# Softplus of the first feed-forward: the logarithm tile in two PSUM banks, in turn, in place of SBUF

## The chip, the cores and the metric

One core of one Trainium2 chip runs the whole program. The metric is the time of one execution on the device in microseconds (us); the median of three runs counts.

## The reference, cut to what matters

```python
x = attention(q, k, v, s)                                  # 2304 tokens x 512
h = x @ w_in                                               # 512 -> 2048
g = np.maximum(h, 0.0) + np.log1p(np.exp(-np.abs(h)))      # softplus
x = g @ w_out                                              # 2048 -> 512
xn = x / sqrt(mean(x * x) + 1e-06) * rms_g
out = (silu(xn @ w_gate) * (xn @ w_val)) @ w_out2          # 512 -> 1536 -> 512
```

Matrices reach TensorE as pairs of a rounded high part and a remainder, and every product is three matmuls: high by high, low by high, high by low.

## The kernel before

The program has three stages: attention (to about 315 us), the first feed-forward (to about 794 us) and the second one (to the end). All instructions are recorded in an order that the kernel sets itself: each kind of work has an offset (the tables `OFF`, `OFF1`, `OFF2`), work item number n stands at n plus its offset, and one sort gives the order of every engine's queue. An engine takes its queue strictly in that order.

The first feed-forward works in 96 steps i. A step is one tile of 384 tokens and one block of 128 hidden columns. The first 36 steps do six blocks for each of the six tiles; the other 60 do the ten remaining blocks of each tile. Each step is a chain over three engines, and the letters are used below:

- **h** (PE, `m1_h`, L642 to L644): 12 matmuls of 384 columns into one PSUM bank. The bank comes from the pair `p`, and in every third step from the bank `x1`, so three banks take turns.
- **A, X, U, LN** (ACT, L661, L665, L673, L669): absolute value of h, exp(-|h|), 1+e rounded, and ln(1+e) into the tile `l`, which lies in SBUF and has two buffers.
- **D** (DVE, L677): e becomes (u-1)-e, the rounding error of U, from two SBUF tiles.
- **G** (DVE, L681): e becomes max(h,0)-e, from PSUM and SBUF. It is the last reader of h and frees its bank.
- **AD** (DVE, L685): l becomes l+e, both in SBUF.
- **GH** (ACT, L689) and **GL** (DVE, L694): the high half of l, and the remainder l-gh. In the first six steps GL runs on POOL.
- **Y** (PE, `m1_y`): 12 matmuls with gh and gl, adding into four PSUM banks that a tile keeps over its blocks.

By the offsets the queues read as follows. PE: h(i), Y(i-3), h(i+1), Y(i-2), ... ACT: A(i), X(i), U(i), LN(i), GH(i-1), A(i+1), ... DVE: D(i), GL(i-1), G(i), AD(i), D(i+1), ... Between these stand the conversions of the weights of both feed-forwards from float64, one chunk in about 1.5 steps: ACT L232 and L234, DVE L241 (some chunks), L242, L244 and L246, POOL L252, then for the chunks kept on chip a split (ACT L278, POOL or DVE L284). POOL also splits the inputs (L639) and does the squares and scaling of the norm (L739 to L773).

After the last block of a tile its norm is made: `m1_ssum` (PE, L753 and L754, two matmuls into the bank `o0`), then `m1_inv` (DVE L762 reads `o0`; ACT L763 and L764 take logarithm and exponential; POOL L765 to L768). Five of the six norms fall into the first feed-forward. Before the change nothing else uses `o0` in this stage.

Of the kernel before, what the change touches and what calls it, by code (L numbers as in the profile page):

```python
# [15 lines left out]
ALU = mybir.AluOpType  # L16
# [98 lines left out]
    "ss": 0.96675,  # L115
    "sr": 0.57611,
    "sh": 4.36453,
    "sm": 6.76979,
    "iv": 7.36353,
    "xn": 8.20666,  # L120
    "xr": 0.64747,
    "sh5": 4.81356,
# [18 lines left out]
def attention_moe_kernel(ctx, tc, q, k, v, s, w_in, w_out, w_gate, w_val, w_out2, rms_g, out):  # L141
    nc = tc.nc
# [9 lines left out]
    T = 384  # L152
# [7 lines left out]
    FA = 6  # L160
# [16 lines left out]
    def ps_p(name):  # L177
        return ps.tile([P, 512], F32, tag="p", name=name, bufs=2)

    def ps_1(tag, w=512):  # L180
        return ps.tile([P, w], F32, tag=tag, name=tag, bufs=1)

    def f32(ap):
        return ap.bitcast(F32)
# [11 lines left out]
    ypd = [dram.tile([DM, T], F32, tag=f"yp{t}", name=f"yp{t}") for t in range(NTILE)]  # L196
    xnT = [dram.tile([DM, T], F32, tag=f"xn{t}", name=f"xn{t}") for t in range(NTILE)]

# [1 line left out]
    slots = {}  # L200
    wfd = [dram.tile([2 * F1, P, 512], F32, tag="wf1", name="wf1"),
           dram.tile([3 * F2, P, 512], F32, tag="wf2", name="wf2")]
# [80 lines left out]
        eng = nc.vector if ph == 1 and c >= NA and c % 4 == 3 else nc.gpsimd  # L283
        eng.tensor_tensor(out=w[1], in0=raws.pop((ph, c)), in1=f32(w[0]), op=ALU.subtract)  # L284

# [1 line left out]
    st = {}  # L287

    def setup():
# [189 lines left out]
    def a_n4(p):  # L479
        scale_rows(st["e4", p], st["r4", p])  # L480

    # groups of transposed blocks: (key block, query blocks); the first two feed float32 products
    GRP = [
        [(0, [0, 1, 2])],
        [(1, [1, 2]), (2, [2])],
# [85 lines left out]
    def on_pair(fn, hd):  # L571
# [25 lines left out]
        "XL": lambda: x_load0(),  # L597
        **{f"X{a}": (lambda a=a: x_split(0, a, nc.vector)) for a in range(KD)},
        "H0": lambda: m1_h(0), "H1": lambda: m1_h(1),
    }  # L600

# [1 line left out]
    def x_tile():  # L603
        return pools["m1"].tile([P, T], F32, tag="xr", name="xr", bufs=2)

# [35 lines left out]
    def mm3(o, wh, wl, xh, xl, start, stop):  # L641
        nc.tensor.matmul(o, wh, xh, start=start, stop=False)  # L642
        nc.tensor.matmul(o, wh, xl, start=False, stop=False)  # L643
        nc.tensor.matmul(o, wl, xh, start=False, stop=stop)  # L644

    def m1_h(i):
        v, _, f = STEPS[i]
        w = slots[1, 2 * f]
        xh, xl = [st["xh", v, a] for a in range(KD)], [st["xl", v, a] for a in range(KD)]
        h = ps_1("x1") if i % 3 == 2 else ps_p("h")  # L650
        for a in range(KD):
            c = slice(a * P, (a + 1) * P)
            mm3(h[:, 0:T], w[0][:, c], w[1][:, c], xh[a], xl[a], a == 0, a == KD - 1)
        st["h", i] = h[:, 0:T]

    def m1_tile(tag, bufs, dt=F32):
        return pools["m1"].tile([P, T], dt, tag=tag, name=tag, bufs=bufs)
# [7 lines left out]
        nc.scalar.activation(out=e, in_=e, func=AF.Exp, scale=-1.0)  # L665

    def m1_ln(i):
        l = st["l", i] = m1_tile("l", 2)
        nc.scalar.activation(out=l, in_=st["e", i], func=AF.Ln, bias=1.0)  # L669

    def m1_u(i):
# [18 lines left out]

    def m1_gl(i):
        gl = st["gl", i] = m1_tile("gl", 3, F32R)
        eng = nc.gpsimd if i < FA else nc.vector
        eng.tensor_tensor(out=gl, in0=st.pop(("l", i)), in1=f32(st["gh", i]), op=ALU.subtract)  # L694

    def m1_y(i):
        v, _, f = STEPS[i]
# [75 lines left out]
        nc.gpsimd.tensor_tensor(out=y, in0=y, in1=st["inv", t], op=ALU.mult)  # L773
        nc.sync.dma_start(out=xnT[t][a * P:(a + 1) * P], in_=y)

# [1 line left out]
    def n_load(t, a):  # L777
        xr = st["xr", t, a] = x_tile()
        nc.sync.dma_start(out=xr, in_=xnT[t][a * P:(a + 1) * P])
# [51 lines left out]
                    nc.vector.tensor_copy(out=ob, in_=o[m][:, c])  # L831
                nc.sync.dma_start(out=out[r:r + P, c], in_=ob)

# [1 line left out]
    with tc.manual_schedule():  # L835
        nc.scalar.preload_act_table_set("natural_log_exp_and_others")
        with ExitStack() as es:
# [21 lines left out]
        with ExitStack() as es0:  # L859
# [8 lines left out]
            for i in NS:  # L868
                for nm, fn in (("h", m1_h), ("A", m1_abs), ("X", m1_exp), ("LN", m1_ln), ("U", m1_u), ("D", m1_d),
                               ("G", m1_g), ("AD", m1_add), ("GH", m1_gh), ("GL", m1_gl), ("Y", m1_y)):  # L870
                    if nm != "h" or i > 1:
                        at(i + OFF1[nm], fn, i)
# [8 lines left out]
            for v in sorted({STEPS[i][0] for i in NS}):  # L881
                i = min(i for i in NS if STEPS[i][0] == v)
# [74 lines left out]
```

## Time and profile before

| | |
|---|---|
| median of 3 runs | 1239.92 us (1238.71 to 1243.12) |
| span of the profiled execution | 1242.4 us |
| PE busy over the span | 1176.2 us (95%) |
| DVE busy | 771.7 us (62%) |
| ACT busy | 617.7 us (50%) |
| POOL busy | 471.5 us (38%) |

The profiled execution lies 2.5 us above the median. Busy shares are means over three stages with different limits, so a change inside the first feed-forward is read from that stage alone. In the 40 slices of the page DVE reads 9 tenths or more from slice 12 to slice 24 (about 370 to 780 us), and in the second feed-forward 3 or 4.

### The profile page before, as it was taken

What the parts mean: (1) busy time and instruction counts of PE and PEld (TensorE: products, weight loads), DVE (VectorE), ACT (ScalarE), POOL (GpSimd) and SP (SyncE); (2) the same over time, 40 slices, a digit from 0 to 9 for tenths busy, and PEclk for the clock granted to TensorE, in tenths of its full rate; (3) what the DMA queues carried; (4) which work ended last, traced back from release to release, by engine and by line L of the source; (5) the groups of instructions that cost most, each with busy time, mean ns of one, the idle gap of its engine ahead of it and who ended that gap; (6) DMA issues with size and microseconds to landing.
All of it is one profiled execution on the core that took longest, in us unless ns stands there. A gap on an engine that the chain in (4) does not pass through costs nothing.

```text
span 1242.4 us, 18308 instructions
## 1 busy us (share of the span) xinstructions
PE 1176.2 (95%) x6404; PEld 1042.1 (84%) x6404; DVE 771.7 (62%) x1396; ACT 617.7 (50%) x1467; POOL 471.5 (38%) x487
## 2 busy tenths in 40 slices
PE   4999999999999998999989879999999999999998
PEld 3677777776988888999888768899999999999997
DVE  4666676654699999998999999533333332333322
ACT  2667666665677777866666666442121121212111
POOL 4455655543354544346576776762000000000000
PEclk9999999999899998999999999999999999999999
DMA  9998888753333343544452332331101010010000
GB/s 181 198 192 178 200 193 186 167 131 100 99 129 119 122 139 123 162 140 134 159 165 91 120 101 85 117 97 58 39 14 39 14 39 1 14 39 13 26 1 26
DMA packets 139037, 128.96 MB, mean 104 GB/s; under 512 B 66656, under 2 KB 116352, under 8 KB 138912
## 3 DMA queue, kind: packets, MB, share of 16 engines
q1 hardware_dynamic: 138848, 127.74, 38.6%
q8 instruction: 51, 0.84, 0.3%
q14 instruction: 42, 0.34, 0.1%
q0 software_dynamic: 96, 0.04, 0.0%
HBM read 76.46 MB, written 26.12 MB: 83 GB/s over the span
## 4 chain that ended last, share of the span: by engine, by line
PE 67%; DVE 22%; ACT 4%; issue 3%; DMA 2%; SPq 2%; POOL 1%; DVEq 0%; POOLq 0%; ACTq 0%
DVE gl L694 5%; PE x L539 4%; PE pt L504 4%; PE g L644 4%; PE g L643 4%; PE v L644 4%; PE v L643 4%; PE v L642 4%; PE g L642 4%; PE o L530 4%; DVE l L685 4%; DVE e L677 3%; PE o L818 3%; PE o L819 3%; PE o L817 3%
## 5 line engine op out<-in xcount | busy, mean ns | idle before, releaser
L643 PE MATMUL y<-gl,w 128*128 128x384 f32 x384 | 134.5, 350 | 25.4 <-DVE gl L694 24.1
L252 POOL TENSOR_TENSOR wf<-ur 128x512 int32<-128x512 int32 x68 | 94.3, 1386 | 123.7 <-DVE ur L246 34.1
L802 DVE TENSOR_TENSOR u<-g,u 128x384 f32<-128x384 f32 x71 | 39.5, 556 | 158.9 <-ACT u L801 158.9
L642 PE MATMUL y<-gh,w 128*128 128x384 f32 x384 | 130.8, 341 | 3.1 <-ACT l L669 1.4
L644 PE MATMUL y<-gh,w 128*128 128x384 f32 x384 | 130.6, 340 | 0.0
L472 POOL TENSOR_SCALAR e<-e,r 128x256 f32<-128x256 f32 (+2 forms) x144 | 78.3, 560 | 127.9 <-ACT hl L368 103.1
L804 ACT ACTIVATE gh<-l 128x384 fp32r<-128x384 f32 x72 | 37.8, 524 | 156.0 <-DVE l L803 156.0
L801 ACT ACTIVATE u<-g 128x384 f32<-128x384 f32 x71 | 34.8, 490 | 151.9 <-PE g L644 151.8
L643 PEld LDWEIGHTS y<-gl,w 128*128 128x128 f32 x384 | 73.3, 191 | 36.7 <-DVE gl L694 35.1
L643 PE MATMUL g<-xl,w 128*128 128x384 f32 x284 | 95.6, 336 | 1.8 <-DVE xl L636 1.8
L689 ACT ACTIVATE gh<-l 128x384 fp32r<-128x384 f32 x96 | 49.9, 520 | 93.7 <-DVE l L685 93.5
L642 PE MATMUL g<-xh,w 128*128 128x384 f32 x284 | 95.8, 337 | 0.7 <-ACT xh L635 0.7
L694 DVE TENSOR_TENSOR gl<-l,gh 128x384 fp32r<-128x384 f32 x90 | 93.1, 1035 | 4.5 <-ACT gh L689 0.7
L644 PE MATMUL g<-xh,w 128*128 128x384 f32 x284 | 95.9, 338 | 0.0
L642 PE MATMUL h<-xh,w 128*128 128x384 f32 x256 | 89.2, 348 | 6.8 <-DVE e L681 6.6
L642 PE MATMUL v<-xh,w 128*128 128x384 f32 x284 | 94.9, 334 | 0.0
L644 PE MATMUL v<-xh,w 128*128 128x384 f32 x284 | 94.9, 334 | 0.0
L643 PE MATMUL v<-xl,w 128*128 128x384 f32 x284 | 94.9, 334 | 0.0
L643 PE MATMUL h<-xl,w 128*128 128x384 f32 x256 | 88.4, 345 | 3.5 <-POOL xl L639 3.3
L644 PE MATMUL h<-xh,w 128*128 128x384 f32 x256 | 87.4, 341 | 0.0
L685 DVE TENSOR_TENSOR l<-l,e 128x384 f32<-128x384 f32 x96 | 84.0, 875 | 3.7
L677 DVE SCALAR_TENSOR_TENSOR e<-u,e 128x384 f32<-128x384 f32 x96 | 73.9, 770 | 17.1 <-ACT l L669 17.1
(191 smaller groups left out, 3281.7 us busy)
## 6 DMA issues: line engine op xcount, KB each, us to landing
sk<-hl SPq DMA_DIRECT2D x96, 256.0 KB
raw<-in_moe_w_out_dram SPq DMA_DIRECT2D x28, 512.0 KB
raw<-in_moe_w_in_dram SPq DMA_DIRECT2D x16, 512.0 KB
raw<-in_moe_w_gate_dram SPq DMA_DIRECT2D x12, 512.0 KB
raw<-in_moe_w_val_dram SPq DMA_DIRECT2D x12, 512.0 KB
wf<-wf SPq DMA_DIRECT2D x24, 256.0 KB
wl<-wf SPq DMA_DIRECT2D x24, 256.0 KB
xr<-x SPq DMA_DIRECT2D x28, 192.0 KB
```

The costliest lines, as they stand in the source:

```text
L252: nc.gpsimd.tensor_tensor(out=w.bitcast(I32), in0=u, in1=r3, op=ALU.add)
L472: nc.gpsimd.tensor_scalar(out=e, in0=e, scalar1=r, scalar2=1.0, op0=ALU.mult, op1=ALU.mult)
L504: nc.tensor.transpose(t[:, o:o + P], e[:, EO[ib] + j0:EO[ib] + j0 + P], ident)
L530: nc.tensor.matmul(o[:, IS - w:IS], vn[:, jb, hd, :], x[:, c:c + w], start=(jb == 0), stop=(jb == 2))
L539: nc.tensor.matmul(t[:, 192 - w:192], vs[r, jb, 2 * hd:2 * hd + 2, :].rearrange("p a d -> p (a d)"), x[r, c:c + w], start=(i == 0 and jb = ...
L642: nc.tensor.matmul(o, wh, xh, start=start, stop=False)
L643: nc.tensor.matmul(o, wh, xl, start=False, stop=False)
L644: nc.tensor.matmul(o, wl, xh, start=False, stop=stop)
L677: nc.vector.scalar_tensor_tensor(out=e, in0=st.pop(("u", i)), scalar=-1.0, in1=e, op0=ALU.add, op1=ALU.subtract)
L685: nc.vector.tensor_tensor(out=l, in0=l, in1=st.pop(("e", i)), op=ALU.add)
L689: nc.scalar.activation(out=gh, in_=st["l", i], func=AF.Copy)
L694: eng.tensor_tensor(out=gl, in0=st.pop(("l", i)), in1=f32(st["gh", i]), op=ALU.subtract)
```

## The change

The tile `l` no longer lies in SBUF. LN writes it into a PSUM bank, `o0` in even steps and `x1` in odd ones; AD adds in place there; GH and GL read it there. Since POOL has no way to that memory in this kernel, GL is on DVE in all 96 steps. With `x1` taken, h has the two banks of `p` alone. The sum for the norm still uses `o0`, now between the logarithms of two even steps, and two offsets put the sum and the reading of it earlier (`sm`, `iv`).

```diff
-    "sm": 6.76979,
-    "iv": 7.36353,
+    "sm": 6.05,
+    "iv": 6.75,
...
-        h = ps_1("x1") if i % 3 == 2 else ps_p("h")
+        h = ps_p("h")
...
     def m1_ln(i):
-        l = st["l", i] = m1_tile("l", 2)
+        l = st["l", i] = ps_1(("o0", "x1")[i % 2])[:, 0:T]
...
         gl = st["gl", i] = m1_tile("gl", 3, F32R)
-        eng = nc.gpsimd if i < FA else nc.vector
-        eng.tensor_tensor(out=gl, in0=st.pop(("l", i)), in1=f32(st["gh", i]), op=ALU.subtract)
+        nc.vector.tensor_tensor(out=gl, in0=st.pop(("l", i)), in1=f32(st["gh", i]), op=ALU.subtract)
```

One line falls away, so L694 (GL) is L693 after the change and L762 (reading the sum) is L761.

On DVE the first steps of the stage read before, where GL is on POOL:

```order
L677 SCALAR_TENSOR_TENSOR e<-u,e 128x384
L681 SCALAR_TENSOR_TENSOR e<-h,e 128x384
L685 TENSOR_TENSOR l<-l,e 128x384
L677 SCALAR_TENSOR_TENSOR e<-u,e 128x384
L681 SCALAR_TENSOR_TENSOR e<-h,e 128x384
```

On DVE the same place after the change (names that begin with `o_` and `x_` are tiles in the banks `o0` and `x1`):

```order
L685 TENSOR_TENSOR o_4219<-o_4219,e 128x384
L677 SCALAR_TENSOR_TENSOR e<-u,e 128x384
L693 TENSOR_TENSOR gl<-o_4219,gh 128x384
L681 SCALAR_TENSOR_TENSOR e<-h,e 128x384
L685 TENSOR_TENSOR x_4247<-x_4247,e 128x384
```

One instruction a step is added to DVE's queue here, between D of a step and its G; from the seventh step on it stood there already.

On DVE around the first norm, before (`sq` is written from the sum, `ur` is a weight in conversion):

```order
L681 SCALAR_TENSOR_TENSOR e<-x_6889,e 128x384
L685 TENSOR_TENSOR l<-l,e 128x384
L242 TENSOR_SCALAR ur<-ur 128x512
L244 TENSOR_SCALAR ur<-ur 128x512
L246 SCALAR_TENSOR_TENSOR ur<-raw,ur 128x512
L677 SCALAR_TENSOR_TENSOR e<-u,e 128x384
L694 TENSOR_TENSOR gl<-l,gh 128x384
L762 TENSOR_SCALAR sq<-o_6984 128x384
L681 SCALAR_TENSOR_TENSOR e<-h,e 128x384
```

On DVE around the first norm, after the change:

```order
L685 TENSOR_TENSOR x_6954<-x_6954,e 128x384
L761 TENSOR_SCALAR sq<-o_6975 128x384
L242 TENSOR_SCALAR ur<-ur 128x512
L244 TENSOR_SCALAR ur<-ur 128x512
L246 SCALAR_TENSOR_TENSOR ur<-raw,ur 128x512
L677 SCALAR_TENSOR_TENSOR e<-u,e 128x384
L693 TENSOR_TENSOR gl<-x_6954,gh 128x384
L681 SCALAR_TENSOR_TENSOR e<-h,e 128x384
L685 TENSOR_TENSOR o_7019<-o_7019,e 128x384
```

The reading of the sum stands ahead of a conversion, of D and of GL, where it stood behind them. On ACT the two instructions that follow it (L763 and L764 before) move up by one step with it and stand again between A and X. On PE the two matmuls of the sum stand between the same neighbours as before, behind a Y and ahead of an h, at every norm.

## Rows read from the trace of the kernel before

**Rows 1.** Busy time by stretch; columns: us, then busy us (instructions) per engine.
```profile
core 0: us, PE busy (x) PEld busy (x) DVE busy (x) ACT busy (x) POOL busy (x), PEclk, DMA share, GB/s
336.50:475.50 139.00, 125.23 (x674) 117.35 (x673) 132.09 (x193) 101.05 (x215) 72.06 (x54) 0.98 0.38 124
475.50:534.90 59.40, 59.40 (x337) 59.40 (x337) 54.99 (x85) 47.35 (x99) 21.74 (x17) 0.98 0.50 161
534.90:767.30 232.40, 205.43 (x1114) 194.92 (x1114) 217.73 (x294) 152.09 (x316) 151.00 (x126) 0.99 0.38 121
767.30:794.30 27.00, 24.43 (x137) 23.39 (x136) 20.31 (x28) 16.91 (x34) 19.23 (x16) 1.00 0.45 138
```

**Rows 2.** Timeline of PE, one h and the Y behind it: start us, us, what.
```profile
501.63 0.33 PE L642 MATMUL h<-xh,w 128*128 128x384 f32 x1
...
503.71 0.33 PE L642 MATMUL y<-gh,w 128*128 128x384 f32 x1
```

**Rows 3.** Waits from 320 to 780 us: us in total, times, longest us.
```profile
PEld y L643 <- DVE gl L694: 35.1, 35, 3.7
...
PEld h L642 <- DVE e L681: 9.5, 9, 1.9
...
ACT acc L763 <- DVE sq L762: 6.7, 5, 2.0
```

**Rows 4.** Single lines: count, then ns minimum/median/maximum of one.
```profile
L694 DVE TENSOR_TENSOR gl<-l,gh x90: 545/852/1656, 349.5 to 785.4; 128x384 fp32r<-128x384 f32 x90
...
L685 DVE TENSOR_TENSOR l<-l,e x96: 557/796/1431, 322.6 to 783.7; 128x384 f32<-128x384 f32 x96
...
L677 DVE SCALAR_TENSOR_TENSOR e<-u,e x96: 544/552/1648, 321.4 to 780.1; 128x384 f32<-128x384 f32 x96
...
L681 DVE SCALAR_TENSOR_TENSOR e<-h,e x64: 541/546/560, 322.0 to 777.5; 128x384 f32<-128x384 f32 x64
...
L661 ACT ACTIVATE e<-h x64: 466/472/499, 319.3 to 772.2; 128x384 f32<-128x384 f32 x64
...
L689 ACT ACTIVATE gh<-l x96: 505/525/533, 324.1 to 784.8; 128x384 fp32r<-128x384 f32 x96
```

**Rows 5.** Line L694 (GL) alone by stretch: us, DVE busy (x), POOL busy (x).
```profile
336.50:475.50 139.00, 24.17 (x26) 2.32 (x2) 0.98 0.38 124
475.50:534.90 59.40, 13.72 (x14) 0.00 (x0) 0.98 0.50 161
534.90:767.30 232.40, 52.11 (x46) 0.00 (x0) 0.99 0.38 121
```

**Rows 6.** Line L685 (AD) alone by stretch.
```profile
336.50:475.50 139.00, 24.14 (x29) 0.98 0.38 124
475.50:534.90 59.40, 11.78 (x14) 0.98 0.50 161
534.90:767.30 232.40, 41.40 (x46) 0.99 0.38 121
```

**Rows 7.** Line L677 (D) alone by stretch.
```profile
336.50:475.50 139.00, 19.72 (x28) 0.98 0.38 124
...
534.90:767.30 232.40, 38.98 (x46) 0.99 0.38 121
```

**Rows 8.** Timeline of POOL and DVE where GL meets a conversion.
```profile
500.95 1.48 POOL L252 TENSOR_TENSOR wf<-ur 128x512 int32<-128x512 int32 x1 [7.58 <-ACT gh L689]
...
501.19 1.66 DVE L694 TENSOR_TENSOR gl<-l,gh 128x384 fp32r<-128x384 f32 x1
```

**Rows 9.** Timeline: start of h and its G, in steps 35 and 46.
```profile
480.83 0.33 PE L642 MATMUL x<-xh,w 128*128 128x384 f32 x1
...
489.07 0.55 DVE L681 SCALAR_TENSOR_TENSOR e<-x,e 128x384 f32<-128x384 f32 x1
...
526.59 0.34 PE L642 MATMUL h<-xh,w 128*128 128x384 f32 x1
...
535.22 0.54 DVE L681 SCALAR_TENSOR_TENSOR e<-h,e 128x384 f32<-128x384 f32 x1
```

## Prediction

> **What bounds the kernel now.** The busy slices of the page come first: outside the first feed-forward the change touches nothing, so its stage alone is read, in the table of busy time by stretch [rows 1]. The stretches begin at the first matmul of steps 6, 34, 48 and 94, so they hold 28, 14 and 46 steps, as the counts of one line per step show [rows 5, 7]. That gives periods of 139.0/28 = 4.96 us, 59.4/14 = 4.24 us and 232.4/46 = 5.05 us a step. What PE needs is read from two starts at full rate: h at 501.63 and Y at 503.71 lie 2.08 us apart, 12 matmuls [rows 2], so a step costs PE 4.16 us. The middle stretch runs at that rate; the other two lose 0.80 and 0.89 us a step. DVE is busy 132.1 of 139.0 us and 217.7 of 232.4 us there, 95 and 94%, and 4.72 and 4.73 us a step [rows 1]; ACT stands at 73 and 65%, POOL at 52 and 65%. The waits say the same: the weight load of Y's second matmul waits 35.1 us for GL on DVE, and h waits 9.5 us for G, the reader that frees its bank [rows 3]. The granted clock is 0.98 or 0.99 in these stretches [rows 1], so almost all of the loss is waiting. DVE sets the pace in two of three stretches.
>
> Why DVE needs so long stands in the single lines: GL takes 545 ns at least but 852 in the median, AD 557 and 796, D up to 1648, while G, of the same size but with one input in PSUM, never leaves 541 to 560 [rows 4]. In the timeline a POOL addition runs from 500.95 to 502.43, and a GL that starts at 501.19 takes 1.66 us instead of 0.56: it stands still until POOL is done [rows 8]. So DVE instructions with two SBUF inputs wait for POOL, and those with one in PSUM don't.
>
> **Terms of the change.** *AD and GL read PSUM.* I take 0.56 us for each, as for G. In the first stretch GL took 24.17 us for 26 and AD 24.14 for 29 [rows 5, 6]: 24.17 - 26 x 0.56 = 9.6 and 24.14 - 29 x 0.56 = 7.9, together 17.5 us; two GLs come over from POOL, +1.1, so 16.4 us net, 0.59 a step. In the last: 52.11 - 25.8 = 26.3 and 41.40 - 25.8 = 15.6, 42.0 us or 0.91 a step. In the middle: 13.72 + 11.78 - 28 x 0.56 = 9.8 us, 0.70 a step. DVE's need falls to (132.1 - 16.4)/28 = 4.13 us and (217.7 - 42.0)/46 = 3.82 us a step.
>
> The Trainium skill (SBUF — State Buffer, "Who interferes with whom") says that DVE's second input from SBUF goes through an interface that it shares with GpSimd, and that an instruction with at most one SBUF input does not contend. G's constant time agrees; by that rule the whole wait of AD and GL goes, as taken here.
>
> *The write into PSUM.* No row shows DVE or ACT writing there. For AD the near end is G, 0.546 us, which reads there [rows 4]; the far end is what AD takes now, 41.40/46 = 0.90 us [rows 6]. I take the near end, since reading there costs nothing extra; at the far end 0.34 us a step stays. LN lies between 0.47 (A, reading PSUM) and 0.53 (GH) [rows 4], GH gains up to 0.05: nothing, both beside DVE's work.
>
> The Trainium skill (ScalarE: Activation LUTs, "Step-by-step: what each stage is for") holds that ScalarE is quicker into PSUM than into SBUF and that VectorE sits closer to SBUF, which speaks for LN and against AD; it gives no figure, and no run here shows either.
>
> *Waits that come back.* D and the conversions still have two SBUF operands or none in PSUM, and the same POOL work (72.1 and 151.0 us, [rows 1]) is squeezed into less time. What GL and AD no longer wait, the next such instruction may. Bounds: nothing comes back, or all. D's wait now is (19.72 - 28 x 0.55)/28 = 0.15 us and (38.98 - 46 x 0.55)/46 = 0.30 us a step [rows 7], so one more instruction beside it catches about a quarter of what the two lose: I take a quarter, +0.15 and +0.23. DVE then needs 4.28 and 4.05.
>
> *Two banks for h instead of three.* h(i) now waits for G(i-2), not G(i-3). From the start of h to the end of G must therefore fit into two periods. In the middle stretch, where PE is never held up, that path is 489.07 + 0.55 - 480.83 = 8.8 us in step 35 and 535.22 + 0.54 - 526.59 = 9.2 in step 46 [rows 9]; over the twelve steps from the one to the other it averages 9.3. The path holds one GL and one AD, so it loses the 0.70 us above: 8.6 us, 4.30 a step. This is above PE's 4.16: the two banks, not PE, become the limit, and the cover that hid the path, a third bank, is gone. Behind a late h stand A, X, U, LN and GH on ACT and D on DVE, and behind those Y. In the loaded stretches the path carries the waits that come back, in two steps: 8.6 + 0.3 = 8.9 and 8.6 + 0.46 = 9.06 us, so 4.45 and 4.53 a step. (Paths of 12 to 17 us stand there now, but they are DVE's queue, which a held h no longer fills.)
>
> *GL of the first six steps onto DVE.* Six times 0.56 is 3.4 us on DVE while it is not yet full; bounds 0 and 3.4, I take half, +1.7.
>
> *The sum of the norm in `o0`.* PE's two matmuls now wait for the GL of the last even step, with h behind them in PE's queue; the next even LN waits for DVE to read the sum. ACT waits 6.7 us in five such places already, 2.0 at most [rows 3], and the third bank covered it. Now it lies on the path: 5 x 1.3 = +6.7. Bounds: 0 if the earlier place hides it, 5 x 2.0 and as much again for ACT's two instructions behind it, some 16 us.
>
> **The sum**, against the span of 1242.4: first stretch 28 x (4.96 - 4.45) = -14.3; middle 14 x (4.30 - 4.24) = +0.8; last 46 x (5.05 - 4.53) = -23.9; norms +6.7; first steps +1.7. Together -29.0, so 1213.4. That execution lies 2.5 us above the median, so I forecast 1211 us. Stall after stall would be late in this order: h behind G first, Y behind GL after.
>
> **Rivals.** *B, PE becomes the bound.* If the path shrinks with DVE's queue (in the middle stretch DVE was still 93% busy, so part of its 8.6 us is queue) it fits into 8.3 and PE runs at 4.2: 28 x 0.76 + 46 x 0.85 - 2 = 58 us less, 1182. For it: DVE's 4.05 to 4.28 leaves it near. Against it: conversions of three or four instructions stand between GL and G in every third step, and the norms.
>
> *C, the waits move.* By the same mechanism that stalls GL, D and the conversions could take up two thirds instead of a quarter: +0.40 and +0.61 a step, paths of 9.4 and 9.8, periods 4.70 and 4.91. Then 28 x 0.26 + 46 x 0.14 - 9 = 5 us less, 1235. For it: POOL's work is unchanged and D already takes 1648 ns at times. Against it: GL, G and AD follow each other without such a wait and give POOL 1.6 us a step of its own. That the new tiles wait for POOL too, so that the change does not do what it says, ends here as well.
>
> The Trainium skill's page SBUF — State Buffer says that the second to issue blocks until the first is done; D and the conversions keep falling under that, which is this rival's mechanism.
>
> *D, slower: the two banks.* The point from which it decides is a path of 9.9 to 10.1 us in the loaded stretches, twice today's period. One of the twelve undisturbed paths is 10.15 us. If the loaded ones come to 10.6, the period is 5.3: 28 x 0.34 + 46 x 0.25 + 8 = 29 us more, about 1269. Against it: GL and AD give 0.6 to 0.9 us of each path back.
>
> **How the numbers follow.** About 0.3% or 4 us is what a measurement of this kernel can tell from no change. The forecast, with its unknown terms (a tenth of a us a step is 7 us, the norms 0 to 16, AD's write), spans 1196 to 1226: chance 0.58. B, 1174 to 1196: 0.20. C, 1226 to 1242: 0.12. D, 1244 to 1275: 0.10. The range leaves out D and the faster half of B: 1184 to 1240. Faster takes the forecast, B and half of C: 0.84; same the rest of C: 0.05; slower D and a little of C: 0.11.
>
> **What the profile would show.** GL and AD at 0.54 to 0.57 us with no spread (a spread up to 1.6 speaks for C's second form); AD above 0.6 says the write costs. D's median above 0.55, and L242's mean higher: waits came back, and how many. In the list of waits h should wait for G far longer than 9.5 us in total, and Y for GL far less than 35.1; if h hardly waits, it is B, and if h waits for 50 us and the periods stand above 5, it is D. PE's two matmuls of the sum and ACT's L763 show the norms' price. Periods of 4.45 and 4.53 between the same steps test the path. I am wrong altogether if DVE is no longer full and h and Y both still wait, as then another engine, ACT with its 65 to 73%, holds the chain.

## The result, and the profile after

The changed kernel takes 1248.18 us in the median of four runs (1246.28 to 1249.67). Set against the kernel before on the same chip the ratio is 1.0057 [1.0036, 1.0078]: slower by some 7 us, or 0.6%, where 1211 was forecast. Ratios here and below leave out single executions that stood far above the others of their kernel. The profiled execution has a span of 1247.5 us, 5.1 above that of before.

The list of busy times says that the change did what it was made for:

```profile
PE 1177.3 (94%) x6404; PEld 1051.3 (84%) x6404; DVE 706.3 (57%) x1402; ACT 616.8 (49%) x1467; POOL 445.6 (36%) x481
```

DVE gave back 65 us of its 771.7. Where they came from is seen line by line (nanoseconds least/median/greatest, then start of the first and the last), and they answer to [rows 4]:

```profile
L693 DVE TENSOR_TENSOR gl<-o,gh x48: 543/546/559, 324.2 to 787.4; 128x384 fp32r<-128x384 f32 x48
L685 DVE TENSOR_TENSOR o<-o,e x48: 566/566/567, 322.9 to 785.4; 128x384 f32<-128x384 f32 x48
L677 DVE SCALAR_TENSOR_TENSOR e<-u,e x96: 545/853/1649, 321.8 to 786.0; 128x384 f32<-128x384 f32 x96
```

GL and AD lost their spread: the greatest of 48 is 16 ns above the least, where GL alone reached 1.66 us [rows 4, 8]. The other 48 of each, in the bank `x1`, are alike (543 to 560 and 566 to 567). D, which keeps two SBUF operands, went the other way, from 552 to 853 in the median.

The busy time by stretch is cut at the first matmul of the same steps as in [rows 1], so again 28, 14 and 46 steps:

```profile
core 0: us, PE busy (x) PEld busy (x) DVE busy (x) ACT busy (x) POOL busy (x), PEclk, DMA share, GB/s
337.95:481.10 143.15, 126.52 (x674) 123.65 (x674) 112.92 (x191) 100.60 (x215) 64.71 (x52) 0.94 0.39 124
481.10:541.50 60.40, 58.89 (x337) 58.11 (x337) 49.39 (x86) 46.25 (x98) 18.79 (x16) 1.00 0.49 158
541.50:775.00 233.50, 206.16 (x1114) 199.34 (x1113) 179.33 (x296) 153.92 (x321) 141.05 (x127) 0.96 0.37 120
```

DVE is busy 112.92/143.15 = 79% and 179.33/233.50 = 77%, where it stood at 95 and 94%. So it no longer sets the pace by its own work, and yet the periods are 143.15/28 = 5.11, 60.44/14 = 4.32 (481.09 to 541.53, which the row rounds) and 233.50/46 = 5.08 us a step, none of them shorter than before. The waits (us in total, times, longest us, from 320 to 800 us) show what took DVE's place, and they answer to [rows 3]:

```profile
ACT e L661 <- PE h L644: 79.3, 75, 3.2
PEld h L642 <- DVE e L681: 55.2, 34, 4.3
PE h L642 <- DVE e L681: 44.5, 27, 4.0
DVE ur L242 <- ACT ur L232: 41.7, 32, 3.9
DVE e L677 <- ACT o L669: 25.6, 26, 4.3
...
PEld y L643 <- DVE gl L693: 0.7, 1, 0.7
```

Y's wait for GL fell from 35.1 us to 0.7. In its place h waits 55.2 us for G, the reader that frees its bank, where it waited 9.5, and 1.5 in the bank `x1`, which the list before the change holds under the name x. And DVE now stands idle for things that PE feeds: D waits for LN, and a conversion waits for its first part on ACT. PE waits for DVE and DVE, by way of ACT, for PE.

### The profile page after: what moved, and what is told of

Same layout as the page of the kernel before. It is cut to its first block, busy times and chain, and to the rows that moved or that the text cites. A ratio compares the mean times of both kernels' runs of the same rounds, so it can differ in the third digit from the quotient of the medians.

```text
span 1247.5 us, 18293 instructions
## 1 busy us (share of the span) xinstructions
PE 1177.3 (94%) x6404; PEld 1051.3 (84%) x6404; DVE 706.3 (57%) x1402; ACT 616.8 (49%) x1467; POOL 445.6 (36%) x481
## 4 chain that ended last, share of the span: by engine, by line
PE 82%; DVE 8%; ACT 5%; issue 2%; SPq 2%; DMA 1%; POOL 0%; DVEq 0%; ACTq 0%
PE h L642 5%; PE x L539 4%; PE h L644 4%; PE h L643 4%; PE pt L504 4%; PE g L644 4%; PE g L643 4%; PE v L642 4%; PE v L643 4%; PE v L644 4%; PE g L642 4%; PE o L530 4%; PE y L642 3%; PE y L643 3%; PE y L644 3%; PE o L817 3%
## 5 line engine op out<-in xcount | busy, mean ns | idle before, releaser
L642 PE MATMUL h<-xh,w 128*128 128x384 f32 x384 | 138.1, 360 | 44.7 <-DVE e L681 44.5
L252 POOL TENSOR_TENSOR wf<-ur 128x512 int32<-128x512 int32 x68 | 90.3, 1329 | 134.1 <-DVE ur L246 71.3
L643 PE MATMUL h<-xl,w 128*128 128x384 f32 x384 | 134.1, 349 | 2.1 <-POOL xl L639 2.1
L644 PE MATMUL h<-xh,w 128*128 128x384 f32 x384 | 133.9, 349 | 0.0
L643 PE MATMUL y<-gl,w 128*128 128x384 f32 x384 | 129.9, 338 | 0.4 <-DVE gl L693 0.4
L642 PEld LDWEIGHTS h<-xh,w 128*128 128x128 f32 x384 | 76.0, 198 | 55.7 <-DVE e L681 55.2
L803 ACT ACTIVATE gh<-l 128x384 fp32r<-128x384 f32 x72 | 37.8, 524 | 156.0 <-DVE l L802 156.0
L677 DVE SCALAR_TENSOR_TENSOR e<-u,e 128x384 f32<-128x384 f32 x96 | 88.4, 921 | 36.6 <-ACT o L669 25.6
L661 ACT ACTIVATE e<-h 128x384 f32<-128x384 f32 x96 | 47.1, 490 | 79.4 <-PE h L644 79.3
L643 PEld LDWEIGHTS h<-xl,w 128*128 128x128 f32 x384 | 76.2, 198 | 3.0 <-POOL xl L639 2.7
L639 POOL TENSOR_TENSOR xl<-xr,xh 128x384 fp32r<-128x384 f32 x44 | 49.1, 1116 | 80.0 <-ACT xh L638 80.0
```

Of the source, the lines that this page charges most:

```text
L252: nc.gpsimd.tensor_tensor(out=w.bitcast(I32), in0=u, in1=r3, op=ALU.add)
L639: eng.tensor_tensor(out=xl, in0=xr, in1=f32(xh), op=ALU.subtract)
L661: nc.scalar.activation(out=e, in_=st["h", i], func=AF.Abs)
L677: nc.vector.scalar_tensor_tensor(out=e, in0=st.pop(("u", i)), scalar=-1.0, in1=e, op0=ALU.add, op1=ALU.subtract)
```

## The experiments

Two theories were set against each other. T1: the two banks hold the kernel, because h(i+2) may not start before G(i) is done. T2: the number of banks is of no account; the order of DVE's queue, or the waits that came back on it, hold the kernel.

**Two banks alone.** The kernel before, with h in the pair `p` at every step and all else as it was.

```diff
-        h = ps_1("x1") if i % 3 == 2 else ps_p("h")
+        h = ps_p("h")
```

> The kernel before with one line changed: h takes the two banks of p in every step, x1 stays unused; the logarithm stays in SBUF and GL where it was. Theory 1 (the third bank of h is what the change lost): DVE keeps its 4.7 us a step and h is now held as well, so the period of the loaded stretches goes from about 5.0 to 5.5 or more, 1275 to 1300 us. Theory 2 (the waits for POOL only moved to D and the conversions, and the bank did not matter): within 5 us of before, about 1240.

Measured: 1268.99 us, ratio 1.018 [1.0133, 1.0226]. T2's 1240 is out, and T1's range is missed by 6 us on the near side. The rows of this kernel come from a second profile of it.

> The kernel of e1_two_banks again, for a profile: h from two banks, all else as before. Theory 1: DVE busy 90% or more of the loaded stretches with GL and AD at 0.9 to 1.1 us as before, and beside that h waits for G by 40 us or more, where it waited 16; periods of 5.2 to 5.4.

Measured: 1268.71 us, span 1266.8. The waits for G, and the busy times of the first and the last stretch:

```profile
PEld h L642 <- DVE e L681: 74.6, 44, 4.3
PE h L642 <- DVE e L681: 60.8, 40, 4.0
```

```profile
337.00:485.00 148.00, 128.48 (x666) 124.59 (x667) 124.75 (x188) 101.25 (x211) 69.55 (x53) 0.92 0.37 118
547.00:780.00 233.00, 199.33 (x1060) 192.33 (x1059) 209.07 (x283) 149.84 (x307) 144.21 (x122) 0.95 0.37 119
```

From first matmul to first matmul the period is 5.31 us in both stretches. DVE's work is about the old one, 4.48 and 4.76 us a step against 4.72 and 4.73, but its share falls from 95 and 94% to 84 and 90%, the first under the 90% expected: here too it stands idle while h waits. The 16 us of the expectation adds the wait of the weight load, 9.5, to that of the matmul behind it, 6.6, which is mostly the same time; for the weight load alone 9.5 became 74.6. The third bank is worth 1.8% by itself.

**Three banks and the relief of DVE.** The kernel before, but G writes into h's own bank, AD adds LN's result (still in SBUF) there, and GH and GL read there. DVE gets the same relief as by the change, h keeps its ring of three banks (each now held until GL), and the norm keeps `o0` and its old place.

```diff
-        nc.vector.scalar_tensor_tensor(out=e, in0=st.pop(("h", i)), scalar=0.0, in1=e, op0=ALU.max, op1=ALU.subtract)
+        nc.vector.scalar_tensor_tensor(out=h, in0=h, scalar=0.0, in1=st.pop(("e", i)), op0=ALU.max, op1=ALU.subtract)
...
-        nc.vector.tensor_tensor(out=l, in0=l, in1=st.pop(("e", i)), op=ALU.add)
+        nc.vector.tensor_tensor(out=h, in0=h, in1=st.pop(("l", i)), op=ALU.add)
...
-        nc.scalar.activation(out=gh, in_=st["l", i], func=AF.Copy)
+        nc.scalar.activation(out=gh, in_=st["h", i], func=AF.Copy)
...
-        eng.tensor_tensor(out=gl, in0=st.pop(("l", i)), in1=f32(st["gh", i]), op=ALU.subtract)
+        nc.vector.tensor_tensor(out=gl, in0=st.pop(("h", i)), in1=f32(st["gh", i]), op=ALU.subtract)
```

> The relief of DVE without the loss of the bank: G writes its result into the bank of h, AD adds the logarithm (which stays in SBUF) there, GH and GL read there. GL and AD thus have one operand in PSUM as in the change, h keeps three banks as before, each held until GL instead of G; o0 is left to the norm, whose offsets are those of before. Theory 1: from h to the end of GL the changed kernel takes 12.4 to 12.7 us on average, three PE steps are 12.5, so some waiting stays: periods of 4.5 to 4.9, 1205 to 1235 us, faster than before. Theory 2: 1240 to 1250, as GL and AD cost the same as in the change.

Measured: 1197.53 us, ratio 0.9612 [0.9574, 0.965], 7 us below T1's range. Its waits, now for GL, and the stretches of the same 28 and 46 steps:

```profile
PEld h L642 <- DVE gl L693: 20.4, 15, 2.4
PE h L642 <- DVE gl L693: 15.5, 13, 2.1
```

```profile
336.20:459.60 123.40, 118.61 (x674) 116.22 (x672) 106.88 (x190) 98.01 (x214) 64.74 (x51) 1.00 0.44 141
518.20:726.40 208.20, 197.70 (x1114) 193.94 (x1113) 180.44 (x296) 153.05 (x321) 143.58 (x127) 0.99 0.41 134
```

DVE's work in these stretches, 107 and 180 us, is about that of the changed kernel, 113 and 179. The relief is the same, the time is 4.5% shorter (1.0057 against 0.9612), and the periods are 4.41 and 4.53.

These kernels make a table of two by two, by their ratios to the kernel before, each taken on its own chip: three banks with DVE's old load 1, two banks with it 1.018, two banks with the relief 1.0057, three with it 0.9612. The relief is worth 1.2% with two banks and 3.9% with three; the third bank is worth 1.8% without the relief and 4.5% with it. The norm is in two of these differences, the 1.2% and the 4.5%, since of the four only the changed kernel makes its sum in a bank that the logarithm shares; that costs about 1% (below).

**A shorter path in two banks.** The changed kernel, with G put ahead of the conversions and of GL in DVE's queue.

```diff
-    "G": 0.93713,
+    "G": 0.53000,
```

> The changed kernel with one offset moved: G stands right behind its D, ahead of GL of the step before and of the conversions and evacuations that stood between GL and G. Theory 1 (two banks of h, with what stands on DVE between D and G on the path): the path from h to G falls from 9.0 us to about 7, under the 8.3 us of two PE steps in most steps, h hardly waits, the period falls from 5.1 to 4.3 or 4.5, 1195 to 1215 us. Theory 2 (DVE only moved its waits): no more than 5 us from the changed kernel's 1248.

Measured: 1214.75 us, ratio 0.9747 [0.9709, 0.9785], inside T1's range, though the path falls to 7.7 and 8.2 us and not to 7, and the period of the last stretch, 4.75, lies above the 4.5 expected. The wait of h for G halves:

```profile
PEld h L642 <- DVE e L681: 27.7, 21, 3.4
PE h L642 <- DVE e L681: 21.3, 17, 3.1
```

The same number in the kernel before tells whether this is DVE's order as such, or the ring.

> The kernel before with the same one offset as e2_g_first: G right behind its D, ahead of GL and the conversions. Theory 1 (order on the path matters because two banks leave no slack, and before DVE itself is full): with three banks h waits 16 us in all, and DVE has the same work, so 1230 to 1245 us, within 1% of before. Theory 2 (the order of G was bad in itself, and e2_g_first owes its gain to that and not to the banks): it gains here as there, 2 to 3%, 1205 to 1215.

Measured: 1239.14 us, ratio 0.9973 [0.9956, 0.999]: hardly anything, as T1 wants. With three banks and a full DVE nobody waited long for G; Y waits for GL as before (37.0 us against 35.1):

```profile
PEld y L643 <- DVE gl L694: 37.0, 29, 2.6
```

So an early G is worth 3.1% with two banks and DVE relieved (1.0057 against 0.9747), and 0.3% where the ring is not the bound.

**The norm.** The changed kernel, without the two matmuls of the sum in the first five norms; DVE reads an SBUF tile in place of the bank. The result of these norms is so left out of the computation, while all the instructions behind it stay.

```diff
-        o = ps_1("o0") if t < NTILE - 1 else ps_p("ss")
+        if t < NTILE - 1:
+            st["ss", t] = f32(sh)
+            return
+        o = ps_p("ss")
```

> The changed kernel without the sum over partitions of the five norms in this stage: its two matmuls are left out and DVE reads an SBUF tile of the same size in its place, so o0 belongs to the logarithm alone; the other instructions of the norm stay where they are. If the norms cost the 7 us of the forecast's term, 1239 to 1243; if they are the main part of the lost time, 1220 to 1230; if they cost nothing, 1247.

Measured: 1237.78 us, ratio 0.9957 [0.9939, 0.9974]. Against the 1.0057 of the changed kernel that is 1.0% or 12 us, between the 7 us of the forecast's term and what would make the norms the main part. Ten matmuls at 2.08/12 = 0.17 us [rows 2] are 1.7 of it. The waits in the last stretch, of the changed kernel first and of this one behind it, and this one's row for the stretch:

```profile
PEld h L642 <- DVE e L681: 31.5, 20, 3.7
...
ACT acc L762 <- DVE sq L761: 8.5, 4, 2.5
```

```profile
PEld h L642 <- DVE e L681: 28.1, 20, 3.0
```

```profile
541.00:764.00 223.00, 199.19 (x1106) 192.21 (x1105) 177.48 (x295) 153.92 (x321) 141.95 (x127) 0.99 0.39 125
```

It is not one long wait at the norm: the wait for G falls by a ninth only. The paths in this stretch are shorter by 0.27 us in the mean (8.69 against 8.96), and the period by 0.23. Of the 10.5 us by which the stretch is shorter, only 3.5 are idle time of PE (233.50 - 206.16 = 27.3 against 223.00 - 199.19 = 23.8). The other 7.0 are its busy time: 1.4 the eight matmuls that are gone, and the rest goes with the granted clock, 0.96 in the changed kernel and 0.99 here. Which wait at the norm brings the clock down there stays open.

**Four banks.** The form of the three-bank kernel, with `o0` as a fourth bank for h. First the sum of the norm alternates between `o0` and `x1`, at its new place:

```diff
-        h = ps_1("x1") if i % 3 == 2 else ps_p("h")
+        h = ps_p("h") if i % 2 == 0 else ps_1(("x1", "o0")[i // 2 % 2])
...
-        o = ps_1("o0") if t < NTILE - 1 else ps_p("ss")
+        o = ps_1(("o0", "x1")[t % 2]) if t < NTILE - 1 else ps_p("ss")
```

> The same with four banks of h in turn (p, x1, p, o0); the norm takes o0 or x1 in turn, with the offsets of the change. Theory 1: four PE steps are 16.6 us, more than nearly all paths from h to GL, so h does not wait but at the five norms; PE or DVE's own work bounds, periods of 4.2 to 4.4, 1185 to 1205 us. Theory 2: no better than e3_in_h_three, 1240 to 1250.

Measured: 1197.46 us, ratio 0.961 [0.9575, 0.9645], inside T1's range and the same as with three. The period of the first stretch falls to 4.25, near PE's 4.16, but that of the last is 4.58, above T1's 4.4. The longest waits of PE there, with either bank, are h behind the reading of the sum (beside them it waits 3.5 us for POOL's split of the inputs, L639):

```profile
PEld x L642 <- DVE sq L761: 5.0, 2, 4.0
PE x L642 <- DVE sq L761: 4.3, 2, 3.7
PEld o L642 <- DVE sq L761: 3.6, 2, 2.6
PE o L642 <- DVE sq L761: 2.9, 2, 2.3
```

The sum takes a bank out of turn, so an h that would have the oldest bank gets the youngest. In the last kernel the sum takes a turn of its own in the same ring of four, at the place that it had before:

```diff
+    def ring():
+        turn[0] += 1
+        k = turn[0] % 4
+        return ps_p("h") if k % 2 else ps_1("x1" if k == 2 else "o0")
...
-        o = ps_1("o0") if t < NTILE - 1 else ps_p("ss")
+        o = ring() if t < NTILE - 1 else ps_p("ss")
```

> As e4_in_h_four (G, AD in the bank of h, held until GL), but the norm's sum takes its place in the same ring of four banks instead of keeping o0 or x1 out of turn, and the norm's offsets are those of before. In e4_in_h_four nearly all lost time lay where h waited for the reading of the sum (periods of 5 to 8 us at ten steps). Theory 1: there h now waits for a GL three steps back at most, periods of 4.2 to 4.4 throughout, 1178 to 1192 us. Rival: the loss at the norms is the chain of DVE, ACT and POOL instructions itself, not the bank: 1192 to 1200.

Measured: 1189.45 us, ratio 0.9586 [0.9562, 0.961], inside Theory 1's range. It is the lowest of all, but its interval touches those of the two kernels before it (0.961 and 0.9612), so the times hardly tell them apart. The period of the last stretch does, 4.33 against 4.58 and 4.53; that of the first is 4.26:

```profile
331.00:450.00 119.00, 118.34 (x678) 116.94 (x676) 107.52 (x188) 97.49 (x212) 65.01 (x51) 1.00 0.43 138
508.00:714.00 206.00, 202.50 (x1152) 199.19 (x1151) 183.68 (x300) 155.85 (x332) 147.76 (x129) 1.00 0.44 139
```

PE is busy 99 and 98% of these stretches at the full clock. This is what the forecast's rival B looked for, PE as the bound: with the relief of DVE four banks in turn were enough for it, and two were not.

## Why the prediction was wrong

**What held.** AD and GL were put at 0.56 us each without spread; they take 0.566 and 0.546. The first six steps cost 1.4 us where 1.7 was taken (the first matmul of step 6 stands at 337.95, before at 336.55). The write into PSUM was put at the near end of its bounds; it costs AD 9 ns over the least that AD took in SBUF [rows 4]. DVE's need was put at 4.28 and 4.05 us a step with the waits that come back, and it is 112.92/28 = 4.03 and 179.33/46 = 3.90. That waits come back on D was right. For D over the whole stage they are this (busy us, mean ns, idle before), against a mean of 770 before:

```profile
L677 DVE SCALAR_TENSOR_TENSOR e<-u,e 128x384 f32<-128x384 f32 x96 | 88.4, 921 | 36.6 <-ACT o L669 25.6
```

That is 0.15 us a step. But the 0.15 and 0.23 of the forecast were for D and the conversions together, and a line of the conversions, before and after the change, gave as much back, against the forecast's sign "L242's mean higher":

```profile
L242 DVE TENSOR_SCALAR ur<-ur 128x512 f32<-128x512 f32 x56 | 43.2, 771 | 5.7 <-ACT ur L232 5.7
```

```profile
L242 DVE TENSOR_SCALAR ur<-ur 128x512 f32<-128x512 f32 x56 | 27.7, 494 | 41.8 <-ACT ur L232 41.7
```

D, L242, L244 and L246 took 191.4 us in all before and 191.8 after, so nothing came back in the sum. Why L242 gained was not tried. Rival C, a DVE full again, is out: DVE stands at 79 and 77%. The path from the start of h to the end of G was put at 8.9 and 9.06 us in the loaded stretches; taken over all steps it is 9.03 and 8.96 in the mean. The mechanism was right too: h behind G in two banks took over from Y behind GL. The measured time lies where rival D was put, 1244 to 1275 with a chance of 0.10, and D's sign came, a wait of some 50 us and periods above 5.

**The step that failed** stands behind these numbers: "so 4.45 and 4.53 a step". It divides the mean path by the two banks. That is right only if every path is alike. The paths of the first stretch run from 6.98 to 12.45 us, and the twelve from which the forecast took its mean ran from 8.60 to 10.15. A path that is longer than two steps of PE, 8.31 us, can hold PE for what it is too long; a path that is shorter gives nothing back, since PE can't run ahead of its own 4.16. So what a step can lose to the banks is the mean of the excess alone. Over 28, 14 and 46 steps, in us a step:

| kernel | mean path | mean excess over the ring | PE idle until G (GL) ends | period less 4.16 |
|---|---|---|---|---|
| changed | 9.03 / 7.94 / 8.96 | 1.00 / 0.36 / 0.99 | 0.59 / 0.11 / 0.54 | 0.95 / 0.16 / 0.92 |
| changed, G early | 7.74 / 6.76 / 8.25 | 0.37 / 0.07 / 0.63 | 0.18 / 0.07 / 0.30 | 0.28 / 0.09 / 0.59 |
| before with two banks | 9.87 / 8.56 / 9.92 | 1.58 / 0.59 / 1.70 | 0.75 / 0.23 / 0.76 | 1.15 / 0.37 / 1.15 |
| three banks, h to GL | 12.24 / 10.92 / 12.28 | 0.44 / 0.05 / 0.61 | 0.17 / 0.00 / 0.23 | 0.25 / 0.02 / 0.37 |

The ring is two steps of PE, 8.31 us, in the first three rows, and three, 12.46, in the last. The first row shows the error: by its means the changed kernel would run at 4.5, and the mean path of the middle stretch, 7.94, lies even below the ring, while 0.16 us a step are lost there. The excess is a bound and not the wait itself. In the loaded stretches PE idles for 0.38 to 0.59 of it, since a PE that has just been held up is late for the next bank anyway: step 14 of the changed kernel has a path of 10.59 us, 2.28 too long, and costs nothing, as PE came to the h of step 16 only at 392.24, when that G had ended at 387.54. The forecast's 4.45 and 4.53 leave 0.29 and 0.37 us a step for this wait, where 0.59 and 0.54 were measured. That the excess of the changed kernel comes out so near its lost time, 1.00 and 0.95, is therefore partly luck. The lost time holds a second part, which the forecast put at nothing: the clock (below).

Against the forecast the loaded stretches are 28 x (5.11 - 4.45) = 18.5 us and 46 x (5.08 - 4.53) = 25.3 us longer, and the norms, which the forecast held apart with 6.7, are in the latter: 37.1 together. By the spans the forecast missed by 1247.5 - 1213.4 = 34.1; what lies behind step 94 ran some 2.7 us shorter than before the change. For rival D the same slip hid the case: "a path of 9.9 to 10.1 us" as the point from which it decides is again a mean, and the change was slower with a mean of 9.0.

**Why paths are so unequal** is seen in step 13 of the changed kernel, one of the two longest paths of its stretch (start us, us, what, idle before):

```profile
380.27 0.56 DVE L726 COPY yt<-y 128x384 f32<-128x384 f32 x1 [2.15 <-PE y L644]
...
380.94 0.34 PE L644 MATMUL y<-gh,w 128*128 128x384 f32 x1
...
381.18 0.66 ACT L232 ACTIVATE ur<-raw 128x512 f32<-128x512 f32 x1
381.32 0.56 DVE L726 COPY yt<-y 128x384 f32<-128x384 f32 x1 [0.49 <-PE y L644]
...
381.79 1.46 DVE L241 TENSOR_SCALAR ur<-raw 128x512 int32<-128x512 uint32 x1
...
383.18 0.41 DVE L242 TENSOR_SCALAR ur<-ur 128x512 f32<-128x512 f32 x1
...
384.09 0.69 DVE L246 SCALAR_TENSOR_TENSOR ur<-raw,ur 128x512 int32<-128x512 int32 x1
384.70 0.55 DVE L681 SCALAR_TENSOR_TENSOR e<-h,e 128x384 f32<-128x384 f32 x1
...
385.30 0.69 PE L642 MATMUL h<-xh,w 128*128 128x384 f32 x1 [4.02 <-DVE e L681]
```

The step's h began at 372.80. G, its last reader, stands in DVE's queue behind the copies of the finished Y (L726), which wait for PE's last matmul at 380.94, and behind a whole conversion. So G ends at 385.25 and the h of step 15 has waited 4.02 us. The forecast named the conversions as its argument against rival B, and then left them out of the division. Before the change DVE was late enough that whatever stood ahead of G in its queue was mostly ready when its turn came; a DVE with time to spare waits in order for PE, and PE waits for it. The early G shows that this order counts: it takes 1.3 us from the mean path of the first stretch and 3.1% from the time.

**The norms** were forecast at 6.7 us more than before. Measured is what their sums in `o0` cost the changed kernel in all, 12 us, 10 without the matmuls themselves; what they cost before the change was not, so the term itself stays open. Its bounds, 0 to 16, are not contradicted; the value was taken from ACT's wait at the old place alone. Their old place in the order was not tried with the change.

**The clock** was not in the sum at all, and this is the second thing that failed. The granted clock fell from 0.98 and 0.99 in the loaded stretches [rows 1] to 0.94 and 0.96. Windows around the wait of step 15 show how:

```profile
377.00:381.00 4.00, 4.00 (x25) 3.96 (x23) 1.58 (x3) 1.63 (x5) 0.26 (x1) 1.00 0.04 15
381.00:385.30 4.30, 0.28 (x2) 0.00 (x0) 3.88 (x7) 3.05 (x7) 2.34 (x3) 0.89 0.68 231
385.30:389.50 4.20, 4.20 (x13) 4.20 (x14) 2.81 (x5) 0.90 (x2) 3.13 (x3) 0.50 0.53 155
389.50:393.00 3.50, 3.50 (x18) 3.50 (x17) 1.99 (x4) 3.42 (x8) 0.58 (x1) 0.76 0.07 25
```

PE is idle for 4.0 us, and the next 13 matmuls come at 0.50, the lower level of 1.2 GHz: they take 4.2 us, where 12 took 2.08 at the upper one [rows 2]. A mean of 0.94 over 143.15 us, between levels of 1 and 0.5, is 0.12 x 143.15 = 17 us at the lower one, against 0.04 x 139 = 5.6 before; in the last stretch 18.7 against 4.6 (from rounded means, so good to a few us). Time at the lower level costs at most its half, so these 26 us more cost at most 13.

In the changed kernel as a whole this is lost beside the waits for G and not inside them. In the first stretch 28 x 0.95 = 26.6 us are lost, but PE is idle for 143.15 - 126.52 = 16.6 only; the rest is in its busy time. The three-bank kernel, at 1.00 and 0.99, needs 118.61 and 197.70 us of PE for the same 674 and 1114 matmuls, the changed one 126.52 and 206.16: 7.9 and 8.5 us more, 16 of the 69 that the loaded stretches lose. Before the change PE's busy time was nearly as high, 125.23 and 205.43 [rows 1], but with more and shorter stops: at the upper level 60 matmuls, most of them behind a stop, added 15 us to PE's time beyond the usual 0.17 each, where 28 add 7 now. So the change turned shorter stops, mostly for GL, into longer ones, for G, and behind a long one the clock was low, as the windows show.

## What to carry to other kernels

Ask of a ring of buffers how long each one is held in single steps, not in the mean: the producer can lose up to the mean of what each hold is too long, and a short hold gives nothing back. Where the producer is TensorE, count the clock too: behind the long stops of this kernel it was at the lower level. Buffers that go to another tile are taken from such a ring, so write the result back into the buffer that already holds the input, where the last reader is on the engine that writes it; here that gave 3.9% where the other form lost 0.6%. And when an engine that was full becomes free, look at what stands in its queue ahead of the instruction that frees the buffer, and whether that waits for the very engine which the buffer holds up.

## What the runs showed of the hardware

ACT is a little quicker with these banks than with SBUF at either end. LN of 128 x 384 takes 477 ns into PSUM and took 510 into SBUF; GH takes 486 from `o0` and 476 from `x1`, and took 525 from SBUF. The Trainium skill (ScalarE: Activation LUTs, "Step-by-step: what each stage is for") says that ScalarE is quicker into PSUM; the trace agrees, by 33 ns. It was worth nothing here, since ACT does not set the pace.

What the other inputs cost beside POOL is larger than any of that. With one operand in PSUM AD never left 566 to 567 ns in 96 instructions, while D, with both in SBUF, ran from 545 to 1649 beside it. The Trainium skill (SBUF — State Buffer, "Who interferes with whom") says that a DVE instruction with two SBUF inputs contends with a GpSimd instruction that reads SBUF, and that one with at most one SBUF input does not, outside the modes that use two ports; for AD, GL, G and D the trace agrees. Two inputs are not the only case, though: L242 reads one SBUF tile, 128 x 512, and before the change it took 419 ns in the mean where it met no POOL instruction and 1176 where it did (30 and 26 of the 56 in this stage). What AD and GL no longer wait was not simply gained by all: 0.15 us a step came back on D, and as much went from L242.
